# Second FFN: tiles 10 and 11 turned by transposing transfers, and tile 4's join moved ahead of two operand splits on GpSimd

## The chip, the core and the metric

The kernel runs on one core of a Trainium2 chip. The metric is the device time of one execution in microseconds (us); lower is better. Five engines work from queues of their own, each in program order, and wait for each other by semaphores: TensorE (PE in the profile; PEld are its weight loads), VectorE (DVE), ScalarE (ACT), GpSimd (POOL) and SyncE (SP), which here issues the transfers (DMA).

## The reference, cut to what matters

Attention gives 1536 tokens of 512 values, a first FFN follows, and then the second FFN, which is the part that the change touches:

```python
def _moe2_ref(x, w_in, w_out, g_ln):          # x: 1536 x 512, w_in: 512 x 1024, w_out: 1024 x 512
    h = x @ w_in
    e = np.exp(h - np.max(h, axis=-1, keepdims=True))
    sm = e / (np.sum(e, axis=-1, keepdims=True) + 1e-09)
    solu = h * sm
    mu = np.mean(solu, axis=-1, keepdims=True)
    var = np.mean((solu - mu) ** 2, axis=-1, keepdims=True)
    ln = (solu - mu) / np.sqrt(var + 1e-06) * g_ln
    return (ln @ w_out).astype(np.float32)
```

## The kernel before, in words

The order of the work is written out by hand: each engine gets its instructions in the order in which the code calls the `emit_` functions. The second FFN works on 12 tiles of 128 tokens (tile t), in 6 pairs (pair p holds tiles 2p and 2p + 1).

**First product.** `emit_m` makes a pair's `h` from seven products (numbered 1 to 7) of 6 matmuls each, in four PSUM banks; every fp32 operand is split into a rounded high half and the remainder (the low half), and three matmuls make one product of such operands. `split_xo` makes the left operands `xo` of a pair, a cast (line 886) and a subtraction (line 887) each, on GpSimd where it is called with `nc.gpsimd`; some of its sources are sums `xsum` from `sum_xo`. `emit_u2`, `emit_u3`, `emit_t5` and `emit_block` put the products together on VectorE.

**Between the products.** For each tile, `emit_exp2` takes the exponential on ScalarE, `emit_mult2` multiplies on VectorE (line 952), `emit_stats` and `emit_factors` take mean and variance on VectorE, with one power on GpSimd (line 975), and `emit_scaled` scales the whole tile `e` on VectorE (line 980).

**Turning.** The second product needs the tile with its 1024 features on the partitions. There are two ways. `turn` does it on TensorE: 8 transposes into two PSUM banks (line 1007), then two copies on ScalarE for the high half (line 1008) and two subtractions on VectorE for the low half (line 1009), into the operand tiles `ls`. The other way is `emit_planes` and `emit_join`. `emit_planes` writes the tile on ScalarE as planes of 16-bit words (line 1023, two instructions) and has SP issue two transposing transfers (line 1026). `emit_join` puts the words together on ScalarE (line 1036, one for each half of the features), makes the high half on ScalarE (line 1040) or as a cast on GpSimd (line 1042), and the low half on GpSimd (line 1043). Tiles 0, 1, 10 and 11 take the first way, 2 to 9 the second.

**Second product.** `emit_o2` makes 24 matmuls for a tile (line 1066): for each of 8 blocks of features high by high, high by low, then low by high, so the third matmul of a half of the features is the first that needs `ls`'s low half. `emit_out` copies the result on ScalarE (line 1076) and stores it; `emit_last` does tile 11 in two halves of the columns with 24 matmuls each.

**Buffers.** The joined words `s` and the sums `xsum` share three buffers in turn; `planes` and `turned` (the transfer's target) share three others, two for each tile; `ls` has four places, tile t using place t mod 4.

Of the kernel before, what the change touches and what calls it, by code (L numbers as in the profile page):

```python
# [29 lines left out]
def as32(t):  # L30
    return t.bitcast(F32)
# [3 lines left out]
def fused_kernel(  # L35
# [14 lines left out]
    nc = tc.nc  # L50
# [60 lines left out]
    class Weights:  # L111
# [119 lines left out]
        def turn(self):  # L231
            self.split()
            self.rebias()
            self.finish()
            self.bits()
# [499 lines left out]
    with tc.manual_schedule():  # L735
# [106 lines left out]
        NPT = NTT // 2  # L842
# [29 lines left out]
        def split_xo(p, which, hi):  # L872
            Xt, f0 = X[2 * p // TPB], 2 * p % TPB * P
            for i in which:
                t = xo_of[p, i] = xpools[p % 2].tile([P, 2, TB], F32R, tag="xs", name="xo")
                n = TB // 2 if i == 3 else TB
                high, low = (t[:, k, 0:n] for k in range(2))
                if i in (0, 3):
                    z = Xt[:, :, f0 + P:f0 + 2 * P] if i == 0 else Xt[:, KC // 2:KC, f0:f0 + P]
                    high, low = (x.rearrange("p (c s) -> p c s", s=P) for x in (high, low))  # L880
                else:
                    z = z_of[p][i - 1]
                if hi is nc.scalar:
                    nc.scalar.activation(out=high, in_=z, func=AF.Copy)
                else:
                    hi.tensor_copy(high, z)  # L886
                nc.gpsimd.tensor_tensor(out=low, in0=z, in1=as32(high), op=ALU.subtract)  # L887
# [15 lines left out]
        banks_of, max_of, p1_of, u2_of, u3_of, t_of, rest = {}, {}, {}, {}, {}, {}, {}  # L903
# [5 lines left out]
        def emit_u2(p):  # L909
            u2_of[p] = conv.tile([P, TB], F32, tag="b", name="u2", bufs=2)  # L910
            nc.vector.tensor_tensor(out=u2_of[p], in0=banks_of[p][BANK[6]], in1=p1_of[p], op=ALU.add)
# [26 lines left out]
        def sides(t, e):  # L938
            p, i = divmod(t, 2)
            return [(banks_of[p][2 * n + 1 - i], e[:, n * 512:(n + 1) * 512]) for n in range(2)]  # L940

        def emit_exp2(t):
            st = max_of[t]
            e = e_of[t] = tail.tile([P, DFF2], F32, tag="e", name="e")
            for k, (h, to) in enumerate(sides(t, e)):
                nc.scalar.activation(out=to, in_=h, func=AF.Exp, bias=st[:, 0:1], accum_out=st[:, 5 + k:6 + k])

        def emit_mult2(t):
            st, e = max_of[t], e_of[t]
            parts = sides(t, e)  # L950
            for h, to in parts:
                nc.vector.tensor_tensor(out=to, in0=h, in1=to, op=ALU.mult)
            if len(parts) == 2:
                nc.vector.tensor_tensor(out=st[:, 5:6], in0=st[:, 5:6], in1=st[:, 6:7], op=ALU.add)
# [3 lines left out]
        def emit_stats(t):  # L958
            bn = tail.tile([P, DFF2 // 512, 6], F32, tag="bn", name="bn")
            for n in range(DFF2 // 512):  # L960
                nc.vector.bn_stats(out=bn[:, n, :], in_=e_of[t][:, n * 512:(n + 1) * 512])  # L961
            mv_of[t] = bn

        def emit_factors(t):
            st, bn = max_of[t], mv_of[t]
            mv = mv_of[t] = tail.tile([P, 2], F32, tag="mv", name="mv")
            nc.vector.bn_aggr(out=mv, in_=bn.rearrange("p n s -> p (n s)"))

            nc.vector.tensor_scalar_add(st[:, 1:2], st[:, 5:6], 1e-9)
            nc.vector.reciprocal(out=st[:, 2:3], in_=st[:, 1:2])  # L970
            nc.vector.tensor_scalar(
                out=st[:, 3:4], in0=mv[:, 1:2], scalar1=st[:, 2:3], scalar2=st[:, 2:3],
                op0=ALU.mult, op1=ALU.mult)
            nc.vector.tensor_scalar_add(st[:, 3:4], st[:, 3:4], 1e-6)
            nc.gpsimd.tensor_tensor(out=st[:, 4:5], in0=st[:, 3:4], in1=mhalf, op=ALU.pow)

        def emit_scaled(t):
            st, mv, e = max_of.pop(t), mv_of.pop(t), e_of[t]
            nc.vector.tensor_tensor(out=st[:, 4:5], in0=st[:, 4:5], in1=st[:, 2:3], op=ALU.mult)
            nc.vector.tensor_scalar(  # L980
                out=e, in0=e, scalar1=mv[:, 0:1], scalar2=st[:, 4:5],
                op0=ALU.subtract, op1=ALU.mult)
# [29 lines left out]
        def halves(tile):  # L1012
            return tile.rearrange("p f w -> p (f w)").bitcast(U16)
# [3 lines left out]
        def emit_planes(t):  # L1017
            e = e_of[t].rearrange("p (n f) -> p n f", n=NH)
            src, dst = (conv.tile([P, DFF2 // 2, 2], I32, tag="raw", name=n, bufs=3) for n in ("planes", "turned"))
            turned_of[t] = halves(dst).rearrange("p (n f) -> p n f", n=NH)  # L1020
            planes = halves(src).rearrange("p (n f) -> p n f", n=NH)
            for n in range(NH):
                nc.scalar.activation(
                    out=planes[:, n].rearrange("p (w f) -> p w f", w=2),
                    in_=e[:, n].bitcast(U16).rearrange("p (f w) -> p w f", w=2), func=AF.Copy)
                nc.sync.dma_start(
                    out=turned_of[t][:, n].rearrange("p (c s) -> p c s", s=P), in_=planes[:, n], transpose=True)

        def emit_join(t, halves=(0, 1), hi=nc.scalar):
            planes = turned_of[t]  # L1030
            if 0 in halves:
                ls_of[t] = ls_tiles(t)
            for n in halves:
                l = ls_of[t][n]
                s = conv.tile([P, TB], I32, tag="s", name="s", bufs=3)
                nc.scalar.activation(
                    out=s.bitcast(U16).rearrange("p (s w) -> p w s", w=2),
                    in_=planes[:, n].rearrange("p (w s) -> p w s", w=2), func=AF.Copy)
                if hi is nc.scalar:
                    nc.scalar.activation(out=l[:, 0, :], in_=as32(s), func=AF.Copy)  # L1040
                else:
                    hi.tensor_copy(l[:, 0, :], as32(s))
                nc.gpsimd.tensor_tensor(out=l[:, 1, :], in0=as32(s), in1=as32(l[:, 0, :]), op=ALU.subtract)  # L1043
# [26 lines left out]
        def emit_o2(t, o):  # L1070
            o_of[t] = o
            o2_products(o, t, 0, NF2, slice(0, DM))

        def emit_out(t):
            osb = tail.tile([P, DM], F32, tag="osb", name="osb", bufs=2)
            nc.scalar.activation(out=osb, in_=o_of.pop(t), func=AF.Copy)
            nc.sync.dma_start(out=out[t * P:(t + 1) * P, :], in_=osb)

        def emit_last(banks):

            t = NTT - 1
            osb = tail.tile([P, DM], F32, tag="osb", name="osb", bufs=2)
            for i in range(2):
                cols = slice(i * DM // 2, (i + 1) * DM // 2)
                o = banks[i][:, 0:DM // 2]
                o2_products(o, t, 0, NF2, cols)
                nc.scalar.activation(out=osb[:, cols], in_=o, func=AF.Copy)
                nc.sync.dma_start(out=out[t * P:(t + 1) * P, cols], in_=osb[:, cols])
# [127 lines left out]
        O = banks_of[0]  # L1216
# [51 lines left out]
        O = banks_of[2]  # L1268
# [21 lines left out]
        emit_stats(6)  # L1290
        emit_u2(4)
        emit_factors(6)
        split_xo(5, (2, 3), nc.gpsimd)
        emit_join(4)
        emit_u3(4)
        emit_mult2(7)
        emit_t5(4)
# [6 lines left out]
        O = banks_of[3]  # L1304
# [25 lines left out]
        complete(5, 2, 4, 3)  # L1330


        f, s = 10, 11
        O = banks_of[4]
        emit_o2(6, O[1])
        emit_join(7, (0, 1), nc.gpsimd)
        emit_o2(7, O[3])
        emit_exp2(f)
        emit_exp2(s)
        emit_out(6)  # L1340
        emit_stats(9)
        emit_factors(9)
        emit_mult2(f)
        emit_scaled(9)
        emit_join(f - 2, (0, 1), nc.gpsimd)
        emit_planes(s - 2)
        emit_o2(f - 2, O[0])
        emit_stats(f)
        emit_factors(f)
        emit_out(f - 3)  # L1350
        emit_mult2(s)
        emit_scaled(f)
        emit_join(s - 2, (0, 1), nc.gpsimd)
        emit_stats(s)
        emit_factors(s)
        turn(f, O[1::2])
        emit_out(f - 2)
        emit_scaled(s)
        emit_o2(s - 2, O[2])
        turn(s, O[1::2])  # L1360
        emit_out(s - 2)
        emit_o2(f, O[0])
        emit_out(f)
        emit_last((O[2], banks_of[NPT - 1][0]))


# [47 lines left out]
```

## Time and profile before

| | |
|---|---|
| median of three timed runs | 491.7 us (490.76 to 491.83) |
| the profiled execution | 485.49 us |
| its span, first to last instruction | 483.7 us |
| TensorE busy in the span | 470.6 us (97%) |
| mean granted TensorE clock | 0.996 of full speed |
| last matmul's output copy starts | 480.33 us |

The profile is of one execution. Its times are us from the start of the span. A timeline row gives the start, the length, the engine, the line, the operation with what it writes and reads, and the count of instructions merged in the row; in brackets stands how long the engine was idle ahead of it and what ended the idle time. TensorE's matmuls are pipelined and their ends are modelled, so start to start of neighbouring rows is the better measure there. A full granted clock (1.00) is 2.4 GHz and half of it 1.2 GHz.

### The profile page before, as it was taken

Reading aid. Unit: us, or ns where it says so; the run is one execution under the profiler, and the core shown is the slowest. Engines: PE = TensorE matmul, PEld = TensorE weight load, DVE = VectorE, ACT = ScalarE, POOL = GpSimd, SP = SyncE. Lnnn points to the kernel's source line nnn. Section 1 sums busy time; section 2 is a strip of 40 time slices with the busy share of each in tenths; the row PEclk is TensorE's granted clock in tenths of the full one; section 3 lists DMA queues with packets and bytes.
Section 4 is the critical chain, followed back from the end, with each engine's and each line's share of the span. In section 5 each row is a group of like instructions: output and inputs, shape, how many; then the busy total and the mean of one; then the engine's idle time right before and its main releaser. Section 6 shows DMA issues by size and latency. Waiting matters only on the chain.

```text
span 483.7 us, 8073 instructions
## 1 busy us (share of the span) xinstructions
PE 470.6 (97%) x2915; PEld 387.2 (80%) x2915; DVE 317.5 (66%) x754; ACT 307.9 (64%) x552; POOL 224.7 (46%) x228
## 2 busy tenths in 40 slices
PE   8999999999999999999999999999999999899997
PEld 4888777778888888888888888888888888678886
DVE  4988775664544456556564556656799999976830
ACT  3698888747676865566656555655943469767731
POOL 3689788424322222223233626382107787955530
PEclk9999999999999999999999999999999999989999
DMA  8989775001233222322232022101200042333311
GB/s 240 280 223 248 197 203 143 3 1 44 88 106 112 87 87 93 117 98 87 88 102 88 28 87 89 57 32 38 92 1 1 23 108 66 66 95 81 87 39 49
DMA packets 56935, 45.65 MB, mean 94 GB/s; under 512 B 38336, under 2 KB 49216, under 8 KB 56896
## 3 DMA queue, kind: packets, MB, share of 16 engines
q1 hardware_dynamic: 56896, 45.14, 32.7%
q8 instruction: 23, 0.38, 0.3%
q14 instruction: 16, 0.13, 0.1%
HBM read 36.61 MB, written 3.15 MB: 82 GB/s over the span
## 4 chain that ended last, share of the span: by engine, by line
PE 71%; DVE 10%; POOL 7%; DMA 3%; SPq 3%; ACT 3%; issue 2%; POOLq 0%; ACTq 0%
PE y L319 26%; PE h L277 26%; PE h L1066 9%; PE h L899 4%; DMA vt<-in_v_dram 2%; PE sps L562 2%; POOL xo L887 2%; PE vsum L473 1%; POOL xsum L862 1%; DVE bn L961 1%; POOL xo L886 1%; DVE h L930 1%; PE aps L599 1%; DVE e L980 1%; SPq L445 1%
## 5 line engine op out<-in xcount | busy, mean ns | idle before, releaser
L277 PE MATMUL h<-xs,w 128*128 128x512 f32 x576 | 141.2, 391 | 0.0
L319 PE MATMUL y<-gs,w 128*128 128x512 f32 x576 | 138.1, 389 | 0.0
L319 PEld LDWEIGHTS y<-gs,w 128*128 128x128 f32 x576 | 108.0, 188 | 22.5
L277 PEld LDWEIGHTS h<-xs,w 128*128 128x128 f32 x576 | 107.1, 188 | 21.6
L187 POOL TENSOR_TENSOR w<-s,w 128x512 fp32r<-128x512 f32 x32 | 41.6, 1300 | 100.9 <-ACT w L186 96.1
L286 ACT ACTIVATE r<-h 128x512 int32<-128x512 f32 x48 | 28.7, 598 | 87.0 <-PE h L277 86.9
L291 DVE SCALAR_TENSOR_TENSOR r<-r,h 128x512 f32<-128x512 int32 x48 | 32.9, 686 | 71.1 <-ACT r L286 70.9
L1066 PE MATMUL h<-w,ls 128*128 128x512 f32 (+1 forms) x312 | 68.9, 380 | 2.5 <-POOL ls L1043 2.5
L1066 PEld LDWEIGHTS h<-w,ls 128*128 128x128 f32 x312 | 56.4, 192 | 13.6 <-POOL ls L1043 2.9
L169 DVE SCALAR_TENSOR_TENSOR s<-raw 128x512 int32<-128x512 int32 x48 | 37.5, 780 | 42.9 <-ACT raw L163 41.7
L899 PE MATMUL h<-w,xo 128*128 128x512 f32 x252 | 58.6, 390 | 0.0
L899 PEld LDWEIGHTS h<-w,xo 128*128 128x128 f32 x252 | 47.1, 188 | 9.7
L296 ACT ACTIVATE r<-r,half_pi 128x512 f32<-128x512 f32 x48 | 34.5, 719 | 5.4 <-DVE r L291 5.3
L301 DVE TENSOR_TENSOR h<-h,r 128x512 f32<-128x512 f32 x48 | 33.0, 688 | 4.9 <-ACT r L296 4.8
L307 DVE TENSOR_TENSOR gs<-h,gs 128x512 fp32r<-128x512 f32 x48 | 32.6, 680 | 5.3 <-ACT gs L306 5.3
L770 POOL TENSOR_TENSOR w<-s,w 128x512 fp32r<-128x512 f32 x14 | 17.8, 1291 | 30.9 <-ACT w L769 30.9
L163 ACT ACTIVATE raw<-raw 128x512 int32<-128x512 uint32 x48 | 32.0, 667 | 0.0
L162 ACT ACTIVATE raw<-raw 128x512 f32<-128x512 f32 x48 | 31.9, 666 | 0.0
L306 ACT ACTIVATE gs<-h 128x512 fp32r<-128x512 f32 x48 | 28.2, 588 | 0.4 <-DVE h L301 0.4
L577 POOL TENSOR_TENSOR sm<-sm,mx 128x480 f32<-128x480 f32 x24 | 24.5, 1024 | 8.2 <-DVE mx L573 8.2
L592 POOL TENSOR_TENSOR sm<-sm,ss 128x480 f32<-128x480 f32 x24 | 26.7, 1113 | 0.3 <-ACT at L604 0.2
L562 PE MATMUL sps<-kx,qx 64*64 64x120 f32 x384 | 24.5, 268 | 1.1 <-ACT kx L526 0.7
(104 smaller groups left out, 663.5 us busy)
## 6 DMA issues: line engine op xcount, KB each, us to landing
raw<-in_moe_w_in_dram SPq DMA_DIRECT2D x24, 512.0 KB, 3.6
raw<-in_moe_w_out_dram SPq DMA_DIRECT2D x24, 512.0 KB, 3.2
vt<-in_v_dram SPq DMA_DIRECT2D x16, 240.0 KB, 4.9
kt<-in_k_dram SPq DMA_DIRECT2D x8, 384.0 KB, 5.4
qt<-in_q_dram SPq DMA_DIRECT2D x8, 384.0 KB, 7.1
out_dram<-osb SPq DMA_DIRECT2D x11, 256.0 KB, 2.0
vt<-vm SPq DMA_DIRECT2D x16, 72.0 KB
vt<-in_v_dram SPq DMA_DIRECT2D x16, 48.0 KB, 6.2
```

Of the source, the lines that this page charges most:

```text
L163: nc.scalar.activation(out=lw, in_=lw.bitcast(U32), func=AF.Copy, scale=TOP3)
L169: nc.vector.scalar_tensor_tensor(out=self.f32[i], in0=t[:, :, 1], scalar=3, in1=t[:, :, 0], op0=ALU.logical_shift_left, op1=ALU.bitwise_or)
L187: nc.gpsimd.tensor_tensor(out=w[:, 1, :], in0=f, in1=as32(w[:, 0, :]), op=ALU.subtract)
L277: nc.tensor.matmul(h, lhsT=w[:, a, f * P:(f + 1) * P], rhs=xs_of[tb, c][:, b_, :], start=(m == 0), stop=(m == 3 * KC - 1))
L291: nc.vector.scalar_tensor_tensor(out=r, in0=r.bitcast(I32), scalar=TWO_PI, in1=h_of[step], op0=ALU.mult, op1=ALU.subtract)
L296: nc.scalar.activation(out=r, in_=r, func=AF.Sin, scale=-1.0, bias=half_pi)
L301: nc.vector.tensor_tensor(out=h, in0=h, in1=r, op=ALU.mult)
L307: nc.vector.tensor_tensor(out=gs[:, 1, :], in0=r, in1=as32(gs[:, 0, :]), op=ALU.subtract)
L319: nc.tensor.matmul(y[e], lhsT=w[:, a, e * P:(e + 1) * P], rhs=gs[:, b_, :], start=(f == 0 and i == 0), stop=(f == GF - 1 and i == 2))
L562: nc.tensor.matmul(sps[h, i, :], lhsT=qx[h, t * QT:(t + 1) * QT], rhs=kx[h, t, :], start=True, stop=True)
L899: nc.tensor.matmul(banks_of[p][BANK[m]], lhsT=x[:, a, s0:s0 + P], rhs=w2_of[m, c][:, b_, :], start=c == j == 0, stop=c == 1 and j == 2)
L1066: nc.tensor.matmul(o, lhsT=ls_of[t][f // 4][:, a, s0:s0 + P], rhs=w[:, b_, cols], start=(f == 0 and i == 0), stop=(f == NF2 - 1 and i == 2))
```

## The change

It has two parts. In the stretch of pair 4, `emit_join(4)` is called ahead of `split_xo(5, (2, 3), nc.gpsimd)` instead of behind it. At the end, tiles 10 and 11 are no longer turned by `turn`: `emit_planes` and `emit_join` (with its high half on GpSimd) do it as for tiles 2 to 9, and the calls of the last stretch stand in another order. The output of tile 10 goes to another bank, as does the first half of tile 11's.

```diff
         emit_factors(6)
+        emit_join(4)
         split_xo(5, (2, 3), nc.gpsimd)
-        emit_join(4)
         emit_u3(4)
...
         emit_o2(7, O[3])
-        emit_exp2(f)
-        emit_exp2(s)
-        emit_out(6)
+        emit_exp2(10)
+        emit_exp2(11)
         emit_stats(9)
         emit_factors(9)
-        emit_mult2(f)
+        emit_mult2(10)
         emit_scaled(9)
-        emit_join(f - 2, (0, 1), nc.gpsimd)
-        emit_planes(s - 2)
-        emit_o2(f - 2, O[0])
-        emit_stats(f)
-        emit_factors(f)
-        emit_out(f - 3)
-        emit_mult2(s)
-        emit_scaled(f)
-        emit_join(s - 2, (0, 1), nc.gpsimd)
-        emit_stats(s)
-        emit_factors(s)
-        turn(f, O[1::2])
-        emit_out(f - 2)
-        emit_scaled(s)
-        emit_o2(s - 2, O[2])
-        turn(s, O[1::2])
-        emit_out(s - 2)
-        emit_o2(f, O[0])
-        emit_out(f)
-        emit_last((O[2], banks_of[NPT - 1][0]))
+        emit_join(8, (0, 1), nc.gpsimd)
+        emit_o2(8, O[0])
+        emit_out(6)
+        emit_planes(9)
+        emit_stats(10)
+        emit_factors(10)
+        emit_mult2(11)
+        emit_scaled(10)
+        emit_planes(10)
+        emit_out(7)
+        emit_stats(11)
+        emit_factors(11)
+        emit_join(9, (0, 1), nc.gpsimd)
+        emit_o2(9, O[2])
+        emit_scaled(11)
+        emit_planes(11)
+        emit_out(8)
+        emit_join(10, (0, 1), nc.gpsimd)
+        emit_o2(10, O[1])
+        emit_join(11, (0, 1), nc.gpsimd)
+        emit_out(9)
+        emit_out(10)
+        emit_last((O[3], banks_of[5][0]))
```

On GpSimd, in the stretch of pair 4, as the difference of the two orders (`xo` are pair 5's operands, the first `ls` rows tile 4's low halves, the casts into `ls` tile 5's):

```order
+L1043 TENSOR_TENSOR ls<-s,ls 128x512 x2
 L886 CAST xo<-xsum 128x512
 L887 TENSOR_TENSOR xo<-xsum,xo 128x512
 L886 CAST xo<-X_75 128x256
 L887 TENSOR_TENSOR xo<-X_75,xo 128x256
-L1043 TENSOR_TENSOR ls<-s,ls 128x512 x2
 L1042 CAST ls<-s 128x512
```

Tile 4's two low halves move ahead of the two splits, which then stand between tile 4's join and tile 5's.

On ScalarE, from behind the exponentials of tiles 10 and 11 to the end of the joins, before (`s` are joined words, `osb` output copies of tiles 6 to 9, `planes` tile 9's):

```order
L1076 ACTIVATE osb<-h_4296 128x512
L1036 ACTIVATE s<-turned 128x2x512 x2
L1023 ACTIVATE planes<-e 128x1024 x2
L1076 ACTIVATE osb<-h_4298 128x512
L1036 ACTIVATE s<-turned 128x2x512 x2
L1008 ACTIVATE ls<-h_4296 128x512
L1008 ACTIVATE ls<-h_4298 128x512
L1076 ACTIVATE osb<-h_4295 128x512
```

and in the changed kernel (the four planes in a row are those of tiles 9 and 10, the four joined words at the end those of tiles 10 and 11):

```order
L1036 ACTIVATE s<-turned 128x2x512 x2
L1076 ACTIVATE osb<-h_4296 128x512
L1023 ACTIVATE planes<-e 128x1024 x4
L1076 ACTIVATE osb<-h_4298 128x512
L1036 ACTIVATE s<-turned 128x2x512 x2
L1023 ACTIVATE planes<-e 128x1024 x2
L1076 ACTIVATE osb<-h_4295 128x512
L1036 ACTIVATE s<-turned 128x2x512 x4
```

Tile 8's join moves ahead of tile 6's output copy, tile 10's planes come ahead of tile 7's output copy and tile 9's join, and the copies out of PSUM for tiles 10 and 11 are gone.

On TensorE, the end of the program as the difference of the two orders (`ident,e` are the transposes; the rows of 24 are the second products of tile 9, then tiles 10 and 11):

```order
-L1007 MATMUL h_4296<-ident,e 128x128 x4
-L1007 MATMUL h_4298<-ident,e 128x128 x4
 L1066 MATMUL h_4297<-w,ls 128x512 x24
-L1007 MATMUL h_4296<-ident,e 128x128 x4
-L1007 MATMUL h_4298<-ident,e 128x128 x4
-L1066 MATMUL h_4295<-w,ls 128x512 x24
-L1066 MATMUL h_4297<-w,ls 128x256 x24
+L1066 MATMUL h_4296<-w,ls 128x512 x24
+L1066 MATMUL h_4298<-w,ls 128x256 x24
 L1066 MATMUL h_4490<-w,ls 128x256 x24
```

Nothing is left between the products; their banks change.

## Rows read from the trace of the kernel before

**Rows 1.** Page, part 1: busy us (share of the span) and instructions of each engine.

```profile
PE 470.6 (97%) x2915; PEld 387.2 (80%) x2915; DVE 317.5 (66%) x754; ACT 307.9 (64%) x552; POOL 224.7 (46%) x228
```

**Rows 2.** TensorE's timeline from tile 4 on: start, length, work [idle before <-releaser].

```profile
420.56 0.61 PE L1066 MATMUL h<-w,ls 128*128 128x512 f32 x2
423.69 12.33 PE L1066 MATMUL h<-w,ls 128*128 128x512 f32 x46 [2.51 <-POOL ls L1043]
435.86 9.68 PE L899 MATMUL h<-w,xo 128*128 128x512 f32 x42
445.38 16.49 PE L1066 MATMUL h<-w,ls 128*128 128x512 f32 x72
461.70 1.04 PE L1007 MATMUL h<-ident,e 128*128 128x128 f32 x8
...
468.83 11.46 PE L1066 MATMUL h<-w,ls 128*128 128x512 f32 x72
```

**Rows 3.** Busy time by stretch, header first: attention's end, then round the wait.

```profile
core 0: us, PE busy (x) PEld busy (x) DVE busy (x) ACT busy (x) POOL busy (x), PEclk, DMA share, GB/s
72.00:74.40 2.40, 1.59 (x29) 1.12 (x25) 0.95 (x5) 2.19 (x5) 2.40 (x4) 1.00 0.01 3
74.40:78.00 3.60, 3.60 (x47) 3.18 (x48) 2.12 (x11) 3.28 (x8) 2.03 (x3) 1.00 0.05 9
...
420.50:423.70 3.20, 0.69 (x4) 0.23 (x3) 3.13 (x7) 2.32 (x3) 3.12 (x5) 1.00 0.01 2
423.70:427.00 3.30, 3.30 (x9) 2.58 (x10) 3.13 (x11) 3.30 (x6) 3.22 (x4) 0.55 0.70 157
```

**Rows 4.** Timeline of GpSimd, then ScalarE, round tile 4's join.

```profile
418.30 0.55 POOL L975 TENSOR_TENSOR st<-st,mhalf 128x1 f32<-128x1 f32 x1
418.80 0.61 POOL L886 CAST xo<-xsum 128x512 fp32r<-128x512 f32 x1
419.49 1.31 POOL L887 TENSOR_TENSOR xo<-xsum,xo 128x512 fp32r<-128x512 f32 x1
...
422.37 2.51 POOL L1043 TENSOR_TENSOR ls<-s,ls 128x512 fp32r<-128x512 f32 x2
...
419.79 0.63 ACT L1040 ACTIVATE ls<-s 128x512 fp32r<-128x512 f32 x1
...
423.29 2.56 ACT L1036 ACTIVATE s<-turned 128x1024 uint16<-128x1024 uint16 x2
```

**Rows 5.** Timeline of VectorE, ScalarE, GpSimd, from pair 5 to tile 9's join.

```profile
438.85 0.69 DVE L911 TENSOR_TENSOR u<-h,p 128x512 f32<-128x512 f32 x1 [5.16 <-PE h L899]
...
447.39 1.28 DVE L961 BATCH_NORM_STATS2 bn<-e 128x6 f32<-128x512 f32 x2
...
448.85 0.21 ACT L946 ACTIVATION_READ_ACCUMULATOR e<-h,st 128x1 f32 x1
...
449.54 1.28 DVE L952 TENSOR_TENSOR e<-h,e 128x512 f32<-128x512 f32 x2
...
451.01 0.60 ACT L1076 ACTIVATE osb<-h 128x512 f32<-128x512 f32 x1 [1.96 <-PE h L1066]
...
451.51 2.58 ACT L1036 ACTIVATE s<-turned 128x1024 uint16<-128x1024 uint16 x2
...
452.94 0.61 POOL L1042 CAST ls<-s 128x512 fp32r<-128x512 f32 x1 [2.69 <-ACT s L1036]
...
453.95 1.98 ACT L1023 ACTIVATE planes<-e 128x1024 uint16<-128x1024 uint16 x2
...
457.81 2.76 ACT L1036 ACTIVATE s<-turned 128x1024 uint16<-128x1024 uint16 x2 [0.76 <-DMA turned<-planes]
```

**Rows 6.** VectorE's scaling beside a GpSimd subtraction (tile 8), and alone (tile 9).

```profile
439.99 1.88 DVE L980 TENSOR_SCALAR e<-e,mv,st 128x1024 f32<-128x1024 f32 x1
440.02 1.29 POOL L1043 TENSOR_TENSOR ls<-s,ls 128x512 fp32r<-128x512 f32 x1
...
450.99 0.81 DVE L980 TENSOR_SCALAR e<-e,mv,st 128x1024 f32<-128x1024 f32 x1
```

More of the change, by code (lines that the diff above doesn't have):

```diff
@@ L1330, in fused_kernel @@
         complete(5, 2, 4, 3)
-        f, s = 10, 11
         O = banks_of[4]
```

## The prediction

> **What bounds the kernel now.** I read the engine totals first: TensorE is busy 97% of the span, VectorE 66%, ScalarE 64%, GpSimd 46% [rows 1]. So a gain must be time in which TensorE waits, runs slowly, or does work that can be left out. The timeline of TensorE from pair 4 on has all three in the stretch that the diff touches [rows 2]. The second product of tile 4 starts at 420.56, issues 2 of its 24 matmuls, waits 2.51 us for the low half of `ls` from GpSimd, and its other 22 plus tile 5's 24 take 12.33. Undisturbed, 42 matmuls step in 445.38 - 435.86 = 9.52, or 0.227 each, so 24 take 5.44, 48 take 10.88, and 46 should show as 10.59 (with the 0.16 by which the 9.68 of the 42 exceeds their step). The 12.33 is 1.74 too long, and the table of stretches says why: the granted clock was 1.00 ahead of the wait and 0.55 in the 3.3 us behind it [rows 3]. Start to start, tiles 4 and 5 cost 435.86 - 420.56 = 15.30 where 10.88 would do: **4.42 us are lost there**. Later, 8 transposes by TensorE stand ahead of tile 9's product (for tile 10) and 8 like them ahead of tile 10's (for tile 11) [rows 2].
>
> **Part 1: tile 4's join ahead of the two splits.** Before, GpSimd makes the operands of two splits (a cast and a subtraction each) between 418.8 and 422.4, and only then both low halves of tile 4, 2.51 together [rows 4]. Little but the queue holds them: the second half's input is ready when ScalarE's copy that starts at 419.79 is done, about 420.42, and the first half's before that [rows 4]. After: pow 418.30 to 418.85, the first low half 1.27 to 420.1. TensorE needs it at 420.56 + 2 x 0.227 = 421.0. The second needs ScalarE's 420.42, and VectorE's scaling of tile 6 wants GpSimd's port in that gap, some 0.56 (below), so it runs about 420.7 to 422.0; needed at 423.7. Tile 4's wait is gone, all 2.51 of it, and with it the cause of the slow 1.74.
>
> What is late next is tile 5. The two splits now end later: 422.0 + 0.6 + 1.3 = 424.0 for the first, 425.2 for the second. Tile 5's join has two things behind that. Its scratch `s` reuses the buffer that the first of these splits reads, so ScalarE starts at 424.0 where it started at 423.29 [rows 4]; and its GpSimd steps stand behind the second split. From the start of ScalarE's copy to GpSimd's cast is 452.94 - 451.51 = 1.43 [rows 5], a cast is 0.61 and a low half 1.29 [rows 5, 6], with some 0.07 between: high at 426.0, low at 427.4. TensorE comes to tile 5 at 420.56 + 5.44 = 426.0 and wants the low half at 426.45, so it waits **0.95**. The bounds: 0.65 if the scaling finds the port free elsewhere, 1.35 if the copy slips by another 0.4. The second half is done by 429.3 and wanted at 430.1. The splits feed product 7 of pair 5, some 9 us on, and cost nothing. First stretch: -4.42 + 0.95 = **-3.47**, if the clock stays up. Pair 5 then starts 3.47 earlier. VectorE's first step in pair 5 now comes after 5.16 of waiting for TensorE [rows 5], so it is free to move along, and pair 5 moves as a whole.
>
> **Part 2: tiles 10 and 11 through the transposing transfer.** From the start of tile 6's product (445.38, here +0) TensorE must do five products of 5.44 and tile 11's half-width product, 480.29 - 468.83 - 5.44 = 6.02: 33.2 in all, against 34.9 now. Removing 16 transposes is worth **-1.7** if nothing waits. TensorE then wants tile 9 at +16.3, tile 10 at +21.8, tile 11 at +27.2. What is added per tile: two plane copies on ScalarE (1.98), two transfers on SP, two joining copies on ScalarE (2.58), two casts and two subtractions on GpSimd (3.8); removed are two copies each on ScalarE and VectorE [rows 5, 6].
>
> Whether they come in time I work out along the queues. ScalarE is free of the exponentials at 449.06 = +3.7 and joins tile 8 at once (it came behind tile 6's output copy before), so GpSimd works on tile 8 from +5.1 to +8.9, wanted at +10.9: in time. But that puts GpSimd beside VectorE's scaling of tile 9. That scaling takes 0.81 when GpSimd is idle, as now; where a GpSimd subtraction ran from 440.02 to 441.31 the scaling begun at 439.99 ended at 441.87, 0.56 behind it [rows 6]. The tiny product ahead of the scaling is held the same way. VectorE therefore ends the scaling of tile 9 at about +8.2 instead of +6.4. Behind it, statistics and factors 2.15 (447.39 to 449.54) [rows 5], the product of tile 11 1.3, and the scaling of tile 10 about 1.0: +12.6. Now ScalarE's order matters: tile 10's planes stand ahead of tile 7's output copy and tile 9's join. Planes from +12.6 to +14.5, the copy 0.5 more (0.60, overlapping its neighbours by 0.1), tile 9's join from +15.0; GpSimd's cast at +16.4, high +17.0, low +18.25. TensorE wants them at +16.3 and, two matmuls after the high half came, at +17.45: it waits 0.7 + 0.8 = **1.5 us ahead of and inside tile 9**. Its bounds: 0 if the scaling of tile 9 gets the port at once (1.7 earlier), 2.5 if the scaling of tile 10 is caught too (1.0 later).
>
> In the Trainium skill, "SBUF — State Buffer", section "Who interferes with whom", GpSimd and VectorE share one port pair, held for a whole instruction while the other blocks fully. The 1.88 against 0.81 agrees. Were the port shared instead, the wait ahead of tile 9 would be near 0 and the sum 1.5 lower.
>
> The rest is covered. Half a tile landed 3.9 us behind the start of its planes (457.81 - 453.95, the one arrival that the trace times) [rows 5]. Tile 9 arrives at +12, ScalarE asks at +15.0; tile 10 at +16.5, asked +19.8; tile 11 at +21.3, asked +22.3. GpSimd then ends tile 10 at +25 and tile 11 at +28.7, where TensorE, 1.5 late, wants their second halves at +26 and +30. If these covers went, each late us would cost one. Last stretch: -1.7 + 1.5 = **-0.2**.
>
> **The sum.** -3.47 - 0.2 = -3.7. The profiled execution took 485.49 (span 483.7); the three timed runs have a median of 491.7, 6.2 more, which no row explains. I carry the difference over: 491.7 - 3.7 = **488.0**, with a span near 480.0 in a profile like this one.
>
> **The rivals.** *The clock falls behind a shorter wait.* For it: it fell behind 2.51. Against it: TensorE waited 0.81 of the 2.40 us from 72.0 on and was granted 1.00 there and in the 3.6 us behind [rows 3]. My waits, 0.95 and a broken 1.5, lie between. The price, if it falls, is the measured 1.74: after one wait 489.7, after both 491.5.
>
> The Trainium skill, "TensorE: Matmul & The Clock Gate", Part 1, says that the gate passes half or all of the pulses and nothing between, after how busy the engine has been. By it the price is whole or nothing, 488.0 or 489.7; the 0.81 and the 2.51 agree with that.
>
> *Everything is covered.* The port is free when VectorE comes, and both waits shrink to some 0.25: -4.42 - 1.7 + 0.5, or 486.1. For it: GpSimd is idle half the time. Against: the two scalings meet a queue of GpSimd work that I can name.
>
> *The wait only moves from tile 4 to tile 5*, with its slow clock: the first stretch gives nothing and 491.5 remains. It needs tile 5's low half 1.5 later than worked out; tile 4's own data speak against it, so this is also the case in which the change doesn't do what it says.
>
> *Slower, by the shared port.* If the scalings lose the port at both ends of my bounds, TensorE waits 1.35 at tile 5 and 2.5 at tile 9 and the clock falls behind both: (-4.42 + 1.35 + 1.74) + (-1.7 + 2.5 + 1.74) = +1.2, or 492.9. With the first stretch as said here, it passes the 0.2% bound from a wait of about 2.3 ahead of tile 9 on.
>
> **How the numbers follow.** Forecast 0.48 (488.0); everything covered 0.12; one fall of the clock 0.18; two falls 0.08; the wait moved 0.06; slower 0.08. A measurement of this kernel can tell about 0.2%, or 1.0 us, from no change. Faster by more: 0.48 + 0.12 + 0.18 = 0.78. Within: 0.08 + 0.06 = 0.14. Slower: 0.08. The range reaches from the covered case, 486.0, to behind one fall of the clock and half way into the cases near 491.5: 490.8.
>
> **What would show it.** Part 1 is right if tile 4's 24 matmuls run without a wait and tile 5 shows one near 0.95 that GpSimd's low half ends; wrong if 2 us or more stand there. The clock is read from the stretch behind it: 1.00, or near 0.55. Part 2 is right if tile 9 waits some 1.5 for GpSimd's cast and low half while VectorE's scaling of tile 9 lasts well over 0.81, and tiles 10 and 11 wait for nothing. A wait for a transfer in any of ScalarE's joins would make the covers wrong; a tail shorter than 33.5 from tile 6's start to the last matmul would make the port wrong.

## The result and the profile after

The changed kernel took 485.22 us (median of 20 executions, 483.11 to 490.43). The kernel before, timed beside it, took 490.06 (median of 20, 485.7 to 495.74). The ratio is 0.9913, with a 95% interval of 0.9886 to 0.994: 4.3 us less, between 2.9 and 5.6. The ratio leaves out executions more than 1.5% above the fastest of their kernel, so it isn't the quotient of the two medians. The forecast of 3.7 us less lies in that interval; the forecast time of 488.0 with its range from 486.0 up does not hold 485.22. The profiled execution took 484.54, with a span of 482.8 us.

TensorE's timeline of the changed kernel, from the start of tile 4's product on (start, length, work, idle before), which answers to [rows 2]:

```profile
422.99 5.85 PE L1066 MATMUL h<-w,ls 128*128 128x512 f32 x24
429.22 0.73 PE L1066 MATMUL h<-w,ls 128*128 128x512 f32 x2 [0.37 <-POOL ls L1042]
430.58 5.28 PE L1066 MATMUL h<-w,ls 128*128 128x512 f32 x22 [0.63 <-POOL ls L1043]
435.70 9.68 PE L899 MATMUL h<-w,xo 128*128 128x512 f32 x42
445.22 17.18 PE L1066 MATMUL h<-w,ls 128*128 128x512 f32 x74
463.03 16.47 PE L1066 MATMUL h<-w,ls 128*128 128x512 f32 x94 [0.63 <-POOL ls L1043]
```

The wait of 2.51 in the middle of tile 4 is gone. Tile 5 waits instead, twice: 0.37 for its high half (the cast) and 0.63 for its low half. Tiles 4 and 5 take 435.70 - 422.99 = 12.71 from start to start, where they took 15.30. Pair 5 steps in 9.52 as before. From tile 6's product to the end of the last matmul it is 463.03 + 16.47 - 445.22 = 34.28, where it was 34.91. The transposes are gone, and one wait of 0.63 inside tile 9 has come.

The granted clock (the number behind the five engines' busy times) in the stretch of each wait and in that behind it, answering to [rows 3]:

```profile
428.60:430.60 2.00, 1.00 (x5) 0.32 (x3) 1.86 (x8) 2.00 (x6) 1.92 (x4) 1.00 0.26 58
430.60:434.00 3.40, 3.40 (x15) 2.83 (x16) 1.46 (x5) 1.40 (x5) 2.28 (x3) 1.00 0.21 77
...
461.50:463.10 1.60, 0.97 (x4) 0.37 (x3) 0.00 (x0) 1.57 (x2) 1.52 (x3) 1.00 0.71 215
463.10:466.10 3.00, 3.00 (x13) 2.48 (x14) 0.00 (x0) 3.00 (x5) 1.85 (x3) 1.00 0.48 110
```

It stayed at 1.00, the full 2.4 GHz, behind both.

GpSimd and ScalarE round tile 4's and tile 5's joins, answering to [rows 4]:

```profile
422.20 1.29 POOL L1043 TENSOR_TENSOR ls<-s,ls 128x512 fp32r<-128x512 f32 x1
423.87 1.64 POOL L1043 TENSOR_TENSOR ls<-s,ls 128x512 fp32r<-128x512 f32 x1 [0.38 <-ACT ls L1040]
424.40 2.01 ACT L1023 ACTIVATE planes<-e 128x1024 uint16<-128x1024 uint16 x2 [0.60 <-DVE e L980]
426.15 1.30 POOL L887 TENSOR_TENSOR xo<-xsum,xo 128x512 fp32r<-128x512 f32 x1
426.31 2.58 ACT L1036 ACTIVATE s<-turned 128x1024 uint16<-128x1024 uint16 x2
...
427.87 0.74 POOL L887 TENSOR_TENSOR xo<-X,xo 128x256 fp32r<-128x256 f32 x1
428.56 0.61 POOL L1042 CAST ls<-s 128x512 fp32r<-128x512 f32 x1
429.25 1.28 POOL L1043 TENSOR_TENSOR ls<-s,ls 128x512 fp32r<-128x512 f32 x1
```

Tile 4's low halves (422.20 and 423.87) now come first. The splits follow (the last subtractions at 426.15 and 427.87), and only then tile 5's cast at 428.56. ScalarE starts tile 5's joined words at 426.31, right behind tile 6's planes of 424.40, and while the first split's subtraction still runs until 427.45.

VectorE, GpSimd and ScalarE from tile 9's scaling to its join, answering to [rows 5] and [rows 6]:

```profile
450.77 0.15 DVE L979 TENSOR_TENSOR st<-st 128x1 f32<-128x1 f32 x1
450.91 1.30 POOL L1043 TENSOR_TENSOR ls<-s,ls 128x512 fp32r<-128x512 f32 x1
450.95 1.82 DVE L980 TENSOR_SCALAR e<-e,mv,st 128x1024 f32<-128x1024 f32 x1
...
452.86 2.01 ACT L1023 ACTIVATE planes<-e 128x1024 uint16<-128x1024 uint16 x2 [1.05 <-DVE e L980]
...
457.19 2.00 ACT L1023 ACTIVATE planes<-e 128x1024 uint16<-128x1024 uint16 x2 [2.32 <-DVE e L980]
...
459.58 2.56 ACT L1036 ACTIVATE s<-turned 128x1024 uint16<-128x1024 uint16 x2
...
461.00 0.61 POOL L1042 CAST ls<-s 128x512 fp32r<-128x512 f32 x1 [1.13 <-ACT s L1036]
```

The scaling of tile 9 lasts 1.82 beside GpSimd's subtraction, where it lasted 0.81 alone. Tile 10's planes wait 2.32 for VectorE, tile 7's output copy and tile 9's join stand behind them, and GpSimd's cast for tile 9 starts at 461.00, 15.8 us behind the start of tile 6's product.

### The profile page after: what moved, and what is told of

It reads as the page before. It is cut to its first block, busy times and chain, and to the rows that moved or that the text cites. A ratio compares the mean times of both kernels' runs of the same rounds, so it can differ in the third digit from the quotient of the medians.

```text
span 482.8 us, 8067 instructions
## 1 busy us (share of the span) xinstructions
PE 468.1 (97%) x2899; PEld 384.1 (80%) x2899; DVE 316.2 (65%) x750; ACT 314.3 (65%) x556; POOL 232.1 (48%) x236
## 4 chain that ended last, share of the span: by engine, by line
PE 72%; DVE 8%; POOL 6%; SPq 4%; DMA 3%; ACT 3%; issue 3%; POOLq 0%; DVEq 0%; ACTq 0%
PE y L319 27%; PE h L277 26%; PE h L899 8%; PE h L1066 7%; DMA vt<-in_v_dram 2%; SPq L445 2%; DVE sm L573 1%; PE vsum L473 1%; PE sps L562 1%; DVE bn L961 1%; POOL xo L887 1%; DMA qt<-in_q_dram 1%; POOL ls L1043 1%; SPq L441 1%; PE aps L599 1%
## 5 line engine op out<-in xcount | busy, mean ns | idle before, releaser
L1066 PE MATMUL h<-w,ls 128*128 128x512 f32 (+1 forms) x312 | 67.8, 375 | 1.6 <-POOL ls L1043 1.3
L1066 PEld LDWEIGHTS h<-w,ls 128*128 128x128 f32 x312 | 55.1, 188 | 13.8 <-POOL ls L1043 2.5
L1023 ACT ACTIVATE planes<-e 128x1024 uint16<-128x1024 uint16 x20 | 20.0, 1050 | 12.4 <-DVE e L980 12.4
L1043 POOL TENSOR_TENSOR ls<-s,ls 128x512 fp32r<-128x512 f32 x20 | 26.2, 1310 | 2.5 <-ACT ls L1040 1.3
```

Source lines behind the costliest of these rows:

```text
L1066: nc.tensor.matmul(o, lhsT=ls_of[t][f // 4][:, a, s0:s0 + P], rhs=w[:, b_, cols], start=(f == 0 and i == 0), stop=(f == NF2 - 1 and i == 2))
```

## The experiments

My theory after the result: the two parts add, part 1 by the removed wait and what of it comes back at tile 5, part 2 by the removed transposes less a wait at tile 9. The rest of the difference between the forecast and the measured time is the baseline. Its rivals: the parts gain only together; or the removed wait is worth more than the first profile shows.

Three numbers describe each profile in what follows: where pair 0's first product starts (everything ahead of it is the same in all kernels here), tiles 4 and 5 from start to start, and the last stretch from tile 6's product to the end of the last matmul. "Pair 0 to end" is the span less the start of pair 0.

| profile | pair 0 starts | tiles 4 and 5 | last stretch | pair 0 to end | ratio to before (95%) |
|---|---|---|---|---|---|
| before | 343.96 | 15.30 | 34.91 | 139.7 | |
| b_again | 349.25 | 13.67 | 34.91 | 138.2 | 1.0004 (0.997 to 1.0038) |
| b_third | 347.67 | 15.13 | 34.91 | 139.6 | one execution |
| b_fourth | 345.60 | 15.04 | 34.91 | 139.5 | one execution |
| part1 | 350.83 | 11.74 | 34.91 | 136.3 | 0.9949 (0.9914 to 0.9985) |
| part2 | 348.27 | 13.68 | 34.28 | 137.3 | 0.9994 (0.9952 to 1.0035) |
| changed | 346.36 | 12.71 | 34.28 | 136.4 | 0.9913 (0.9886 to 0.994) |
| a_again | 351.15 | 11.75 | 34.26 | 135.5 | 0.9885 (0.9828 to 0.9942) |
| a_third | 344.10 | 11.75 | 34.28 | 135.4 | 0.9934 (0.9897 to 0.997) |
| mid | 346.40 | 12.55 | 34.30 | 136.3 | 0.9963 (0.9921 to 1.0005) |
| split3 | 349.81 | 11.87 | 33.88 | 135.2 | 0.9932 (0.9896 to 0.9967) |
| join9 | 345.13 | 12.66 | 34.10 | 136.2 | 0.9911 (0.9872 to 0.9949) |
| both | 344.15 | 11.90 | 34.98 | 136.3 | 0.9898 (0.9856 to 0.994) |
| early5 | 345.78 | 10.88 | 34.30 | 134.5 | 0.9919 (0.9878 to 0.9959) |

**The kernel before, again (b_again, b_third, b_fourth; no edit).**

> The kernel before, unchanged, once more. Theory A (the program from tile 4's second product on takes the same time in every execution, and what differs between executions is the start): from the start of tile 4's product to the end of the span 63.1 us again, with a wait of 2.5 us for GpSimd's low half and a slow clock behind it; first matmul of the second FFN's pair 4 at another time than 411.0, later by about as much as the span is longer than 483.7. Theory B (tile 4's wait itself differs between executions, and is longer in the slower ones): a stretch of more than 64.5 us, or a wait other than 2.5 us. Ratio 1.00 for both.

TensorE's timeline of b_again, in the attention and at tile 4, and the stretch behind tile 4's wait:

```profile
54.88 2.78 PE L473 MATMUL vsum<-vt,strip 96*64 96x128 f32 x24 [2.16 <-DMA vt<-in_v_dram]
...
425.91 0.61 PE L1066 MATMUL h<-w,ls 128*128 128x512 f32 x2
429.02 10.72 PE L1066 MATMUL h<-w,ls 128*128 128x512 f32 x46 [2.50 <-POOL ls L1043]
```

```profile
429.02:432.30 3.28, 3.28 (x14) 2.74 (x15) 3.11 (x11) 3.28 (x6) 3.20 (x4) 1.00 0.70 159
```

Both theories were partly wrong. Pair 0 starts 5.3 us later than in the first profile, and the first row shows one place where such time goes: TensorE waits 2.16 for the transfer of an attention operand. Behind that wait the granted clock fell too:

```profile
54.80:58.00 3.20, 3.12 (x28) 2.82 (x30) 0.88 (x4) 0.30 (x2) 3.20 (x4) 0.56 1.02 299
```

That much is theory A. But the rest of the program was not the same. The wait at tile 4 is 2.50 again, yet the 46 matmuls behind it take 10.72 and not 12.33, and the clock stayed at 1.00. So the slow clock behind this wait is no fixed part of it. (One of the 12 executions of b_again took 1203.92 us, which nothing here explains; the ratio leaves it out.) That called for more profiles:

> The kernel before once more, for another profile. Behind tile 4's wait of 2.5 us the clock fell in the first profile (15.3 us for tiles 4 and 5) and not in two others (13.7 us). If it falls in most executions: 0.55 in the 3.3 us behind the wait, 15.3 us. If the first profile was the exception: 1.00 and 13.7 us.

> The same once more: 15.3 us for tiles 4 and 5 with the clock fallen, or 13.7 us without.

TensorE's timeline of b_third, and the stretch behind the wait:

```profile
424.31 0.61 PE L1066 MATMUL h<-w,ls 128*128 128x512 f32 x2
427.41 12.19 PE L1066 MATMUL h<-w,ls 128*128 128x512 f32 x46 [2.49 <-POOL ls L1043]
```

```profile
428.00:431.50 3.50, 3.50 (x12) 2.75 (x11) 3.29 (x13) 3.50 (x9) 3.34 (x5) 0.64 0.46 102
```

Behind the same wait of 2.49 the clock fell here, to a mean of 0.64 over 3.5 us, and in b_fourth too (12.08 for the 46 matmuls). Over the five profiles that have the wait (part2 is the fifth) it fell in three. Tiles 4 and 5 cost 15.0 to 15.3 where it fell and 13.7 where it did not. The mean granted clock of the executions that the ratios count agrees without a profile: 0.9950 over 94 executions of kernels with this wait, 0.9972 over 92 of kernels without it. This mean holds falls in attention too, and the comparison takes these to be as frequent in both groups. The difference of 0.0022 of some 486 us is 1.07 us, about 0.7 of a fall, which cost 1.36 to 1.61 in the three profiles (12.08 to 12.33 less 10.72).

**Each part alone (part1, part2) and together (a_again, a_third).** In part1 the last stretch is as before:

```diff
         emit_factors(6)
+        emit_join(4)
         split_xo(5, (2, 3), nc.gpsimd)
-        emit_join(4)
         emit_u3(4)
```

In part2 this edit is left out, and the last stretch is the changed kernel's.

> Tile 4's join ahead of the two splits alone, with the last stretch as before. My theory: tile 4 and tile 5 together take about 12.7 us from start to start where they took 15.3, so 2.6 us less, with two short waits at tile 5 and the clock at full speed; the last stretch from tile 6's product stays 34.9. Ratio 0.993 to 0.995. Rival (the two parts gain only together, because the last stretch had slack that only the new order uses): 1.00, the gain given back behind pair 5.

> Tiles 10 and 11 by transposing transfers alone, with tile 4's join behind the splits as before. My theory: tile 4 keeps its wait of 2.5 us and the slow clock, 15.3 us for tiles 4 and 5; the last stretch from tile 6's product to the last matmul takes 34.3 where it took 34.9. Gain 0.6 us: ratio 0.998 to 1.000. Rival (the last stretch is worth its full 1.7 us): ratio 0.9965.

> The changed kernel, unchanged, once more, beside its two parts. If the parts add: its ratio is the product of the two, 0.991 to 0.994, and from the start of tile 4's product to the end of the span it takes 59.8 us again. If more than the two parts is in it: a ratio lower than the product by over 0.002.

> The changed kernel once more, beside the kernel before, for a third profile and more runs. From the start of pair 0's first product to the end of the span it took 136.4 and 135.5 us so far, while that start itself stood at 346.4 and 351.2. If only what lies ahead of pair 0 differs between executions: 135.4 to 136.5 again, whatever the span. Ratio 0.988 to 0.994.

TensorE's timeline of part1, and of part2:

```profile
427.47 6.07 PE L1066 MATMUL h<-w,ls 128*128 128x512 f32 x26
434.10 5.28 PE L1066 MATMUL h<-w,ls 128*128 128x512 f32 x22 [0.56 <-POOL ls L1043]
439.21 9.68 PE L899 MATMUL h<-w,xo 128*128 128x512 f32 x42
```

```profile
424.90 0.61 PE L1066 MATMUL h<-w,ls 128*128 128x512 f32 x2
428.02 10.72 PE L1066 MATMUL h<-w,ls 128*128 128x512 f32 x46 [2.50 <-POOL ls L1043]
...
448.10 17.19 PE L1066 MATMUL h<-w,ls 128*128 128x512 f32 x74
465.91 16.47 PE L1066 MATMUL h<-w,ls 128*128 128x512 f32 x94 [0.62 <-POOL ls L1043]
```

Part 1 alone: 11.74 for tiles 4 and 5, with one wait of 0.56 where the first profile of the changed kernel has two, and the last stretch of before to the hundredth. Part 2 alone: tile 4's wait as before, 34.28 in the last stretch. For tiles 4 and 5 both expectations missed: 12.7 with two waits was expected in part1 and 15.3 with the clock fallen in part2 (13.68, and the clock stayed at 1.00). The rival that they gain only together is out: each takes its time where it was put and gives nothing back. The ratios agree as far as they reach. Their product is 0.9949 x 0.9994 = 0.9943, that of a_third is 0.9934. That of a_again, 0.9885, lies 0.0058 below the product, past the 0.002 that the expectation named as a sign of something more; but its interval is wide, a_third doesn't repeat it, and its trace has 11.75 and 34.26 in the two stretches, which is what the parts give. Part 2 by itself can't be told from no change by its ratio; that it is worth 0.63 us rests on the traces.

In a_third, from pair 0 to the end took 135.4, as in a_again (135.5), while the first profile of the changed kernel took 136.4. Tile 5's only wait there:

```profile
427.36 5.28 PE L1066 MATMUL h<-w,ls 128*128 128x512 f32 x22 [0.57 <-POOL ls L1043]
```

The difference of 1.0 lies in tiles 4 and 5 alone (11.75 against 12.71): in the first profile of the changed kernel GpSimd began tile 4's first low half at 422.20, 0.8 ahead of TensorE's first product of that tile at 422.99; in a_again it began 1.8 ahead (426.02 and 427.78), and in part1 too (425.69 and 427.47). Why the two engines stand differently to each other at that point from one execution to the next was not tried.

**How long a wait does the clock survive? (mid)**

```diff
+        split_xo(5, (2,), nc.gpsimd)
         emit_join(4)
-        split_xo(5, (2, 3), nc.gpsimd)
+        split_xo(5, (3,), nc.gpsimd)
```

> The changed kernel with the first of the two splits ahead of tile 4's join and the second behind it, so that tile 4 waits, but for less than before. It asks how long a wait the clock survives. Expected wait at tile 4 about 1.5 us (2.51 less the second split's cast and subtraction). If the clock falls behind any wait over about 1 us: a granted clock near 0.55 in the 3 us behind, and 24 matmuls behind it in more than 6.5 us. If it does not: 1.00, and tiles 4 and 5 in 12.2 to 12.8 us from start to start.

TensorE's timeline and the stretch behind the wait:

```profile
423.03 0.61 PE L1066 MATMUL h<-w,ls 128*128 128x512 f32 x2
425.01 10.73 PE L1066 MATMUL h<-w,ls 128*128 128x512 f32 x46 [1.37 <-POOL ls L1043]
```

```profile
425.01:428.30 3.29, 3.29 (x14) 2.74 (x15) 3.15 (x10) 3.29 (x4) 3.13 (x5) 1.00 0.64 146
```

A wait of 1.37, and the clock stayed at 1.00. In no profile here did it fall behind a wait of 0.4 to 1.4 at these tiles; behind 2.5 it fell three times of five. What lies between was not tried at these tiles, but attention shows it: of the nine waits of 1.6 us or more ahead of pair 0 in the 14 profiles, six have a fall behind them (1.61, 1.67, 1.81, 2.16, 3.49 and 3.82) and three have none (1.62, 2.05 and 2.05). So the length of the wait alone doesn't decide it. Of the 1.67 that tiles 4 and 5 lose in mid (12.55 less 10.88), 1.37 is the wait, so a break costs some 0.3 on top of the idle time that the profile shows. The same reads from b_again (2.79 lost, 2.50 idle) and part1 (0.86 lost, 0.56 idle). Of this, 0.16 is how the ends of matmuls are modelled (42 matmuls show as 9.68 and step in 9.52), and 0.13 to 0.14 is in the matmuls behind the wait (46 in 10.72 or 10.73, where 10.59 would do).

**What does tile 5 wait for? (split3, early5)** In split3 the second split goes behind tile 5's join on GpSimd:

```diff
         emit_join(4)
-        split_xo(5, (2, 3), nc.gpsimd)
+        split_xo(5, (2,), nc.gpsimd)
...
         emit_join(5, (0, 1), nc.gpsimd)
+        split_xo(5, (3,), nc.gpsimd)
```

> The changed kernel with the second of the two splits (a cast and a subtraction of 256 columns, 1.15 us) moved behind tile 5's join on GpSimd. My theory (tile 5 waits because its join stands behind both splits): the wait at tile 5 falls from 0.55 to 1.0 us to 0.2 or less, and tiles 4 and 5 take 10.9 to 11.4 us from start to start where the changed kernel takes 11.75 or 12.7. Rival (tile 5's joined words wait for the buffer that the first split reads, as the prediction said): the wait stays at 0.5 us or more, since ScalarE's copy for tile 5 starts no earlier.

TensorE's and GpSimd's timeline:

```profile
426.45 6.28 PE L1066 MATMUL h<-w,ls 128*128 128x512 f32 x26
433.21 5.28 PE L1066 MATMUL h<-w,ls 128*128 128x512 f32 x22 [0.47 <-POOL ls L1043]
```

```profile
429.61 1.29 POOL L887 TENSOR_TENSOR xo<-xsum,xo 128x512 fp32r<-128x512 f32 x1
431.18 0.61 POOL L1042 CAST ls<-s 128x512 fp32r<-128x512 f32 x1 [0.29 <-ACT s L1036]
```

The wait stayed, at 0.47, and tiles 4 and 5 take 11.87, no less than in a_third (11.75), so my theory had only half of it. GpSimd was free at 430.9 and waited 0.29 for ScalarE's joined words. Not for the buffer, as the rival says: in the changed kernel these words were begun before that buffer was read for the last time. They stand on ScalarE behind tile 6's planes. (The last stretch of split3 is 33.88, 0.4 less than the changed kernel's, although the edit leaves its calls alone; why was not tried, and one profile can't show whether it stays.) So in early5 tile 5's join goes ahead of both queues at once:

```diff
         emit_join(4)
+        emit_join(5, (0, 1), nc.gpsimd)
         split_xo(5, (2, 3), nc.gpsimd)
...
         emit_o2(4, O[1])
-        emit_join(5, (0, 1), nc.gpsimd)
         emit_o2(5, O[3])
```

> The changed kernel with tile 5's join called right behind tile 4's, ahead of both splits and ahead of tile 6's planes on ScalarE. In the changed kernel ScalarE starts tile 5's join only behind tile 6's planes, and GpSimd only behind both splits. If these two queues are what tile 5 waits for: no wait for GpSimd at tile 5, tiles 4 and 5 in 10.9 to 11.2 us from start to start where the changed kernel takes 11.75 or 12.7, and the last stretch 34.3 as there. If something else holds tile 5: a wait of 0.4 us or more remains. If the splits, now last, hold product 7 of pair 5: a wait inside pair 5, whose 42 matmuls then step in more than 9.6 us. Against the changed kernel beside it the ratio would be 0.997 to 0.9985, too little for the intervals of these runs; the traces decide.

TensorE's timeline of early5:

```profile
422.39 11.04 PE L1066 MATMUL h<-w,ls 128*128 128x512 f32 x48
433.27 9.68 PE L899 MATMUL h<-w,xo 128*128 128x512 f32 x42
442.79 17.20 PE L1066 MATMUL h<-w,ls 128*128 128x512 f32 x74
460.61 16.48 PE L1066 MATMUL h<-w,ls 128*128 128x512 f32 x94 [0.62 <-POOL ls L1043]
```

Tiles 4 and 5 run in 10.88 without a break, and pair 5, which now gets its operands last, steps in 9.52 as ever. From pair 0 to the end it took 134.5, 0.9 less than a_third beside it and 3.7 to 5.2 less than the profiles of before. This is the fastest version by the traces, with one profile of it; the ratios (0.9919 and 0.9934, both intervals some 0.004 each way) can't tell the two apart.

**What does tile 9 wait for? (join9, both)**

```diff
         emit_scaled(10)
-        emit_planes(10)
-        emit_out(7)
         emit_stats(11)
         emit_factors(11)
         emit_join(9, (0, 1), nc.gpsimd)
         emit_o2(9, O[2])
+        emit_planes(10)
+        emit_out(7)
```

> The changed kernel with tile 9's join called ahead of tile 10's planes and tile 7's output copy. My theory (tile 9 waits because its join stands behind tile 10's planes, which wait for VectorE's scaling): the two waits of about 0.6 us at tile 9 go, and from tile 6's product to the last matmul it takes 33.2 to 33.5 us where the changed kernel takes 34.3. Rival 1 (tile 9's transfer is not in earlier): the wait stays and ends with a transfer or with ScalarE's join. Rival 2 (tile 10's planes, 2 us later, come too late): a wait of the same size at tile 10 or 11.

TensorE's and ScalarE's timeline:

```profile
443.97 22.44 PE L1066 MATMUL h<-w,ls 128*128 128x512 f32 x98
467.04 11.03 PE L1066 MATMUL h<-w,ls 128*128 128x512 f32 x70 [0.63 <-POOL ls L1043]
```

```profile
455.49 2.75 ACT L1036 ACTIVATE s<-turned 128x1024 uint16<-128x1024 uint16 x2 [1.89 <-DMA turned<-planes]
458.11 1.98 ACT L1023 ACTIVATE planes<-e 128x1024 uint16<-128x1024 uint16 x2
...
461.21 2.01 ACT L1023 ACTIVATE planes<-e 128x1024 uint16<-128x1024 uint16 x2 [0.64 <-DVE e L980]
...
463.60 3.95 ACT L1036 ACTIVATE s<-turned 128x1024 uint16<-128x1024 uint16 x3
```

The wait at tile 9 is gone: the first row now holds 98 matmuls, all of tile 9's among them. But ScalarE now waits 1.89 for tile 9's transfer, and the next tile in the queue, tile 10, waits 0.63 in the same way, since its planes start 2 us later and its join stands behind tile 11's planes. That is my second rival; the stretch gains 0.18. In `both`, with the edit of split3 as well:

> Both moves in one kernel: the second split behind tile 5's join, and tile 9's join ahead of tile 10's planes. If each wait is its own cost: from tile 4's product to the end of the span 57.4 to 58.0 us, where the changed kernel takes 58.8 or 59.8, and a ratio to the kernel before of 0.987 to 0.990. If a wait removed only shows up behind: 58.8 or more.

TensorE's two waits behind tile 6's product:

```profile
459.71 5.81 PE L1066 MATMUL h<-w,ls 128*128 128x512 f32 x24 [0.56 <-POOL ls L1043]
466.14 11.04 PE L1066 MATMUL h<-w,ls 128*128 128x512 f32 x70 [0.62 <-POOL ls L1043]
```

Here the last stretch has two waits (0.56 at tile 9, 0.62 at tile 10) and takes 34.98; a third, of 0.48, stays at tile 5. From tile 4's product to the end it took 59.6, no less than the changed kernel's 58.8 to 59.8. Nothing was gained, as the second case of the expectation has it. Why the wait at tile 9, gone in join9, is back was not tried: VectorE starts tile 9's scaling 6.62 behind tile 6's product here and 5.72 behind it in join9, and with one profile of each the edit can't be told from the execution.

## Why the prediction was wrong, step by step

**The change in time came out within the measured interval; the time did not come out in the range.** The step that failed is the last one: 3.7 us were taken off 491.7, the median of three executions, although the profiled one was at 485.49 and the text itself says that no row explains the 6.2 between them. The runs show how wide such medians lie. Executions of the kernel before ranged from 485.7 to 495.74 in the set of 20, with a median of 490.06, and medians of three later sets of 23 to 29 were 487.7, 488.3 and 488.7. In the profiles the part that varies lies ahead of pair 0, whose start moves from 343.96 to 351.15, with waits for attention's operands, the longest in each profile 0.3 to 3.8 us, and in six of the 14 profiles with a fall of the clock behind one of them. The executions without a profile go the same way: in the 94 executions with tile 4's wait that the ratios count, those with a mean clock of 0.998 or more took 485.4 on average, those at 0.995 to 0.997 took 487.6, those at 0.993 or less 490.2. The three executions behind 491.7 were not profiled, so that it was such a draw is the likeliest reading and not shown for them. The range held the unknowns of the change but not this one. Carried to 490.06, the same sum gives 486.4 and a range of 484.4 to 489.2. Where the start is alike, the forecast holds in a profile: a_third, with pair 0 at 344.10 beside 343.96, has a span of 479.5, where 480.0 was forecast. And the measurement could tell less than the 0.2% that the prediction names: with 20 executions of each kernel, the interval reaches 0.27% to each side.

**Part 1: the removed term.** The wait of 2.51 went as forecast. The 1.74 of slow clock was counted in full, as a cost that the wait always brings. It comes in three profiles of five, and in about 0.7 of the executions by the mean clocks, at 1.36 to 1.61 a time, so on average some 1.0. This term was too large by 0.7.

**Part 1: the new term.** Tile 5 was to wait 0.95; the idle time is 1.00 in the first profile and 0.57 in a_third. What tiles 4 and 5 lose is 1.83 in the one and 0.87 in the other, since each break costs some 0.3 to 0.4 more than its idle time. First stretch: -3.47 forecast; -2.6 between the two first profiles, -3.4 from b_third to a_third, -1.9 from b_again to a_third, where no clock fell. One of the two reasons given was false: tile 5's joined words do not wait for the buffer of the first split. ScalarE began them at 426.31, behind tile 6's planes, and the buffer was read until 427.45, so these words lie in another of the three buffers. That the forecast start (3.4 behind tile 4's product) fell near the one of the first profile (3.3) was luck: in a_third it is 2.3 (423.07 and 420.73). The other reason, the queue behind the second split, holds, but each of the two queues hides the other: moving one (split3) left 0.47, moving both (early5) left nothing.

**Part 2.** The structure was right: 33.2 without waits, a scaling of tile 9 that GpSimd's subtraction holds up (1.82), tile 10's planes ahead of tile 9's join, and a wait at tile 9 as the only one; no join waits for a transfer. The size was off: a wait of 1.5 was worked out, 34.28 - 33.2 = 1.1 was lost. The tiny product ahead of the scaling (450.77, 0.15) was not held, so the scaling ended 7.6 us behind tile 6's start and not 8.2, and GpSimd's cast came at +15.8 and not +16.4. The last stretch gained 0.63 where 0.2 was forecast.

**The sum by the traces.** From tile 4's product to the end of the span: 63.14 before, 59.81 after, so -3.3 where -3.7 was forecast. That the sums lie so near is in part luck: the slow clock was counted 0.7 too high, the last stretch 0.4 too low, and the two errors work against each other.

**The rivals.** The clock did not fall behind any of the shorter waits, up to 1.37. Not everything was covered, and the wait did not move whole to tile 5. Of the two scalings at the ends of the bounds only tile 9's was slowed (1.82); tile 6's lasted 0.81, and only the tiny product ahead of it was longer (0.65, beside 0.15 at tile 9). That the change doesn't do what it says is out by part1 and part2.

## What to carry to other kernels

A difference worked out from two traces belongs to the stretch that it was worked out in. Before it is set against a median, look at how far executions of the same kernel lie apart and which stretch makes that spread; if it is another stretch, its spread belongs in the range. A slow clock behind a wait is a risk with a price, not a part of the wait. And an instruction that waits behind two queues gains only when it is moved ahead of both.

## What the runs showed of the hardware that was not expected

- Behind the same wait of 2.49 to 2.51 us the granted clock fell in three profiles (46 matmuls in 12.08 to 12.33 us) and stayed at full speed in two (10.72).
- In attention the clock fell behind waits of 1.61, 1.67, 1.81 and 2.16 us and stayed at 1.00 behind 1.62 and, twice, 2.05.
- A wait in the middle of a run of matmuls costs about 0.3 us more than the idle time that the profile shows for it (0.56, 1.37 and 2.50 idle; 0.86, 1.67 and 2.79 lost), about half of it by the modelled ends of matmuls.
- The start of pair 0, some 350 us into a program that does the same work each time, moved by 7.2 us between profiles. Waits for attention's transfers are part of it (2.16 in the row of b_again above, 1.23 the longest in a_third, whose pair 0 starts at 344.10), and so are the falls of the clock behind some of them. Why these transfers land at other times from one execution to the next was not tried.
